# The sign of a converted weight: from a pass of its own into the slope of a Prelu

## Chip, cores and metric

The kernel runs on one core of a Trainium2 chip. The metric is the time of one execution on the device in microseconds (us). Its engines are named as in the profile: PE is TensorE's matmul queue and PEld its weight loads, DVE is VectorE, ACT is ScalarE, POOL is GpSimd, SP is SyncE, which issues the DMAs here.

## What is computed

An attention in two stages (32 packed queries per head read keys and values, then the 576 queries of a head read the packed result), whose output goes through two feed-forward layers. The weights of both layers arrive as 64-bit floats and are used as 32-bit floats.

```python
def _attn_ref(q, k, v, p):                       # 8 batches, 8 heads, 576 x 64; p has 32 rows
    p_packed = sm_attn(p, k, v)
    return sm_attn(q, p_packed, p_packed)

def _moe_ref(x, w_in, w_out):                    # x: 4608 x 512; d_ff = 2048
    h = x @ w_in
    return (h - np.tanh(h)) @ w_out

def _moe2_ref(x, w_in, w_out):
    h = x @ w_in
    return (h * np.cos(h)) @ w_out
...
    x = _moe_ref(x=x, **moe_kwargs)
    return _moe2_ref(x=x, **moe2_kwargs)
```

## The kernel before

**Stages.** First comes the attention of batch 0 and the conversion of the first weights (up to some 35 us). Then follow 128 steps of the first layer, up to some 770 us: for each half batch and each pair of hidden chunks PE makes h (`h1`, L517, 12 matmuls), ACT and DVE make h - tanh(h) of it (`el1`, `el2`, L532 to L550), `el3` (ACT, L561) and `el4` (POOL, L565) split the result into a high part gh and a low part gl, and two steps later PE multiplies both by w_out (`ymm1`, L578, 24 matmuls). The attention of the following batch is woven in between: its scores sc and their exponential e (L317, L341), transposes tp (L355), pp, s and so on, and the product gp of the packed result with w_in (`gmat`, L479), which `gsplit` (L493, L498) splits into g. The second layer with the cosine fills the rest of the time; no weight is converted there any more.

**Conversion.** `Conv` turns 64-bit floats into 32-bit floats, 64 tiles of 128 x 512 numbers in all: 32 of the first layer (16 w_in, called w1i, and 16 w_out, called wt and then w1o) up to some 165 us, and 32 of the second layer between 250 and 775 us. A tile st is loaded by SP (L149) as pairs of words. In `a`, ACT scales the high word, read as a 32-bit float, by 2^-112 (L167, Copy): that moves the exponent to the place where a shift left by 3 makes a 32-bit float of it. The sign sits in the topmost bit, and the shift pushes it out. A second ACT pass (L170) makes the three missing low bits from the low word. In `b_ops`, DVE joins both: shift left by 3, or with the low bits (`join`, L208). The sign is put back in one of two ways, chosen for each tile by the letter in `SPLIT` (first layer) and `SPLIT2` (second layer):

- "L": DVE ors the high word's sign bit into the low bits before the join (`sign`, L187). 20 tiles of the first layer, the last 8 of the second.
- "S": a third ACT pass (L175) writes the scaled high word as a 16-bit float, sign included, into the upper half of the low word. 12 tiles of the first layer, the first 24 of the second.

`c` then splits a finished w_out or second-layer tile (ACT L231, POOL L232). `gmat` needs the w1i tiles, `ymm1` the w1o tiles.

**Order.** The attention of batch 0 and, from step 15 on, all steps stand in an order written by hand. For steps 0 to 14 a scheduler orders each engine's queue by its own estimate of the durations. `STEP_A` and `CONV2` say in which steps a conversion is started; inside a step, `el2` weaves the DVE operations of pending conversions (`fill`) between its own four. On ACT a conversion started in a step stands behind that step's y and k (L539, L542) and ahead of what `mid` holds, as the exponential e.

Of the kernel before, what the change touches and what calls it, by code (L numbers as in the profile page):

```python
# [14 lines left out]
U16 = mybir.dt.uint16  # L15
U32 = mybir.dt.uint32
F16 = mybir.dt.float16
BF16 = mybir.dt.bfloat16
AF = mybir.ActivationFunctionType
ALU = mybir.AluOpType  # L20
# [13 lines left out]
    "i2 i0 i3 i1 o1 o0 i4 i5 i6 i7 o3 o4 o2 o5 o7 i8 "  # L34
    "o6 i9 i10 i11 i14 o9 i12 i13 o8 i15 o11 o13 o12 o10 o15 o14"
).split()
SPLIT = "LLSSLLSLLLSLSLSLLSLSLSLSLLSLLSLL"
SPLIT2 = "S" * 24 + "L" * 8
STEP_A = (1, 2, 2, 2, 1, 2, 1, 1, 1, 1, 0, 2, 1, 1, 1, 1, 1, 1, 0, 3, 1, 1)
CONV2 = (34, 35, 37, 38) + tuple(16 * k + r for k in (3, 4, 5, 6) for r in (0, 2, 3, 5, 6))  # L40
CONV2 += (112, 114, 116, 118, 120, 122, 124, 126)
# [29 lines left out]
    11: (13,), 12: (12, 14), 13: (15, 18, 16), 14: (19,), 16: (17,), 17: (20, 21), 18: (22,),  # L71
}
PREP0 = (23, 24, 25)
SGN = -2147483648
LOW_BIAS = -0.5 + 2.0 ** -10


# [1 line left out]
def fused_kernel(ctx, tc, qT, kT, v, pT, w1i, w1o, w2i, w2o, ident, out):  # L79
    nc = tc.nc  # L80
    B, _, _, _, HB = qT.shape
    S = 2 * HB
# [36 lines left out]
    def f32(ap):  # L119
        return ap.bitcast(F32)  # L120
# [10 lines left out]
    class Conv:  # L131
# [20 lines left out]
        def a(self):  # L152
            self.prefetch()
            if not self.ready:
                return
            kind, f, st = self.ready.pop(0)
            way = self.split[self.na]
            self.na += 1
            if kind == "w1i":
                if f // 2 not in w1in:  # L160
                    w1in[f // 2] = wp.tile([128, 2, 512], F32, tag="w", name="w1i")
                w = w1in[f // 2][:, f % 2, :]
            else:
                w = self.alloc_tmp()
            sv = st.rearrange("p (n two) -> p n two", two=2)
            hi, x = sv[:, :, 1], sv[:, :, 0]
            nc.scalar.activation(out=w, in_=f32(hi), func=AF.Copy, scale=2.0 ** -112)  # L167
            halves = st.bitcast(U16).rearrange("p (n four) -> p n four", four=4)
            if way != "D":
                nc.scalar.activation(  # L170
                    out=x, in_=x.bitcast(U32), func=AF.Identity,
                    scale=2.0 ** -29 * (1 - 2.0 ** -11), bias=LOW_BIAS,
                )
            if way == "S":
                nc.scalar.activation(  # L175
                    out=halves[:, :, 1].bitcast(F16), in_=f32(hi), func=AF.Copy, scale=2.0 ** -60
                )
            self.done_a.append((kind, f, hi, w, x, way))

        def b_ops(self):  # L180
            if not self.done_a:
                return []
            kind, f, hi, w, x, way = self.done_a.pop(0)
            wi = w.bitcast(I32)

            def sign():
                nc.vector.scalar_tensor_tensor(  # L187
                    out=x, in0=hi, scalar=SGN, in1=x, op0=ALU.bitwise_and, op1=ALU.bitwise_or
                )

            def shift():
                nc.vector.tensor_scalar(
                    out=wi, in0=wi, scalar1=3, scalar2=None, op0=ALU.logical_shift_left
                )

            def put_sign():
                nc.vector.scalar_tensor_tensor(
                    out=wi, in0=hi, scalar=SGN, in1=wi, op0=ALU.bitwise_and, op1=ALU.bitwise_or
                )

            def join():
                if way == "D":
                    nc.vector.scalar_tensor_tensor(
                        out=wi, in0=x, scalar=29, in1=wi,
                        op0=ALU.logical_shift_right, op1=ALU.bitwise_or,
                    )
                else:
                    nc.vector.scalar_tensor_tensor(  # L208
                        out=wi, in0=wi, scalar=3, in1=x,
                        op0=ALU.logical_shift_left, op1=ALU.bitwise_or,  # L210
                    )
                if kind == "w1i":
                    self.bdone.add(f)
                else:
                    self.done_b.append((kind, f, w))
                if kind[1] == "2":
                    stores.append((raw[kind[2]][f // 2][:, f % 2], w))
                self.prefetch()

            return {"S": [join], "L": [sign, join], "D": [shift, put_sign, join]}[way]  # L220

        def b(self):
            for fn in self.b_ops():
# [425 lines left out]
    def cos_round(a, h):  # L649
        nc.scalar.activation(out=a, in_=h, func=AF.Identity, bias=MAGIC)  # L650

    def cos_frac(a, h):
        nc.vector.scalar_tensor_tensor(
            out=a, in0=a, scalar=MAGIC, in1=h, op0=ALU.subtract, op1=ALU.subtract
        )
# [306 lines left out]

    conv = Conv([("w1" + o[0], int(o[1:])) for o in ORDER], 3, SPLIT, alloc_st, alloc_tmp)

# [74 lines left out]

    conv2 = Conv(todo2, 2, SPLIT2, alloc_st2, alloc_tmp2)  # L1040

# [25 lines left out]
    for n, (blk, s) in enumerate(steps):  # L1067
# [7 lines left out]
        st = {}  # L1075
# [85 lines left out]
    for s in range(NSTEP):  # L1161
        st = st0 if s == 0 else {}
# [70 lines left out]
    def psp():  # L1233
        i = nbank[0] % 4
        nbank[0] += 1
        if banks[i] is not None:
            t, banks[i] = banks[i], None
            return t
        return psx.tile([128, TB], F32, tag=f"p{i}", bufs=1, name="p")
# [78 lines left out]
    for t in pairs:  # L1318
# [23 lines left out]
        for F in range(NSTEP):  # L1342
            w = wfirst if (t, F) == (pairs[0], 0) else None
# [4 lines left out]
            A, C, B = psp(), psp(), psp()  # L1348
# [82 lines left out]
        for k, (p, P) in enumerate(jobs):  # L1431
# [7 lines left out]
            hi, lo = done[k]  # L1439
# [102 lines left out]
```

## Time and profile before

| what | value |
|---|---|
| median of 3 runs | 1495.38 us (1494.09 to 1496.17) |
| profiled execution, its own time | 1494.03 us |
| its span from first to last instruction | 1492.2 us |
| busy in the span: PE, DVE, ACT, POOL | 97%, 79%, 69%, 26% |

A page of the profile holds one execution: the busy time of each engine, the chain of work that ended last (followed back from the end, at each step to what released it), groups of instructions by line with mean duration, and waits with what ended them. A busy PE need not be PE at its peak; the granted clock is given as a share of full speed (1.00 is 2.4 GHz, 0.50 is 1.2 GHz).

### The profile page before, as it was taken

Reading aid. Unit: us, or ns where it says so; the run is one execution under the profiler, and the core shown is the slowest. Engines: PE = TensorE matmul, PEld = TensorE weight load, DVE = VectorE, ACT = ScalarE, POOL = GpSimd, SP = SyncE. Lnnn points to the kernel's source line nnn. Section 1 sums busy time; section 2 is a strip of 40 time slices with the busy share of each in tenths; the row PEclk is TensorE's granted clock in tenths of the full one; section 3 lists DMA queues with packets and bytes.
Section 4 is the critical chain, followed back from the end, with each engine's and each line's share of the span. In section 5 each row is a group of like instructions: output and inputs, shape, how many; then the busy total and the mean of one; then the engine's idle time right before and its main releaser. Section 6 shows DMA issues by size and latency. Waiting matters only on the chain.

```text
span 1492.2 us, 29411 instructions
## 1 busy us (share of the span) xinstructions
PE 1440.5 (97%) x11296; PEld 1305.9 (88%) x11296; DVE 1184.2 (79%) x1562; ACT 1034.6 (69%) x1592; POOL 383.8 (26%) x356
## 2 busy tenths in 40 slices
PE   4789999999999999999999999999999999999998
PEld 2578999989998899988998888998889988998898
DVE  6998787777878788789976778886888688868874
ACT  5899767879788787977875656655665466636652
POOL 0353454554645455454550000000000000000000
PEclk8799999999999999999999999999999999999999
DMA  9642464646647474564669757776668766776656
GB/s 356 217 159 75 144 207 139 226 143 207 211 170 246 159 246 150 198 216 151 196 244 382 247 165 231 231 254 211 206 186 255 220 203 192 237 237 205 182 161 186
DMA packets 179980, 307.67 MB, mean 206 GB/s; under 512 B 14912, under 2 KB 110144, under 8 KB 179840
## 3 DMA queue, kind: packets, MB, share of 16 engines
q1 hardware_dynamic: 179840, 305.79, 62.8%
q8 instruction: 90, 1.47, 0.4%
q14 instruction: 50, 0.41, 0.1%
HBM read 238.35 MB, written 67.37 MB: 205 GB/s over the span
## 4 chain that ended last, share of the span: by engine, by line
PE 77%; ACT 8%; DVE 5%; issue 5%; POOL 3%; DMA 1%; SPq 0%; DVEq 0%; POOLq 0%; ACTq 0%
PE p L899 21%; PE y L578 17%; PE y L909 15%; PE h L517 9%; PE p L909 6%; PE h L639 3%; PE y L715 3%; POOL gl L565 2%; PE gp L479 2%; DVE y L550 1%; ACT u L533 1%; ACT st L175 1%; ACT st L170 1%; ACT y L539 1%; DVE y L546 1%
## 5 line engine op out<-in xcount | busy, mean ns | idle before, releaser
L899 PE MATMUL p<-b,hw 128*128 128x512 f32 x1302 | 310.4, 391 | 0.0
L578 PE MATMUL y<-gh,w1o 128*128 128x288 f32 x2048 | 305.3, 301 | 3.2 <-DVE ye L608 1.0
L578 PEld LDWEIGHTS y<-gh,w1o 128*128 128x128 f32 x2048 | 279.1, 189 | 31.1 <-issue 12.0
L899 PEld LDWEIGHTS p<-b,hw 128*128 128x128 f32 x1302 | 239.1, 188 | 47.0
L565 POOL TENSOR_TENSOR gl<-y,gh 128x576 fp32r<-128x576 f32 x127 | 245.7, 1935 | 22.4 <-ACT gh L561 22.4
L517 PE MATMUL h<-a,g 128*128 128x288 f32 x1536 | 228.8, 298 | 17.8 <-DVE d L545 7.6
L517 PEld LDWEIGHTS h<-a,g 128*128 128x128 f32 x1536 | 212.9, 190 | 21.7 <-ACT st L170 8.2
L532 ACT ACTIVATE t<-h 128x576 f32<-128x576 f32 x128 | 85.3, 667 | 122.9 <-PE h L517 122.8
L578 PE MATMUL y<-gl,w1o 128*128 128x288 f32 x1024 | 157.6, 296 | 5.5 <-POOL gl L565 5.2
L578 PEld LDWEIGHTS y<-gl,w1o 128*128 128x128 f32 x1024 | 142.7, 188 | 9.2 <-POOL gl L565 8.7
L550 DVE COPY_PREDICATED y<-k,t 128x576 f32<-128x576 int16 x128 | 132.4, 1035 | 9.9
L909 PE MATMUL y<-yw,yh 128*128 128x256 f32 x768 | 136.2, 279 | 0.2 <-DMA yw<-wod 0.2
L544 DVE TENSOR_TENSOR t<-h,t 128x576 f32<-128x576 f32 x128 | 95.2, 744 | 51.2 <-ACT u L533 50.7
L909 PEld LDWEIGHTS y<-yw,yh 128*128 128x128 f32 x768 | 117.6, 188 | 0.9 <-ACT o L920 0.4
L546 DVE SCALAR_TENSOR_TENSOR y<-y,d 128x576 f32<-128x576 f32 x128 | 104.0, 813 | 16.9 <-ACT y L539 10.4
L909 PE MATMUL y<-yw,yl 128*128 128x256 f32 x384 | 107.4, 280 | 0.0
L917 DVE TENSOR_TENSOR yl<-k,yh 128x1024 fp32r<-128x1024 f32 x72 | 87.1, 1220 | 23.4 <-ACT yh L920 22.9
L561 ACT ACTIVATE gh<-y 128x576 fp32r<-128x576 f32 x128 | 88.2, 689 | 9.9 <-DVE y L550 9.6
L545 DVE TENSOR_TENSOR d<-u,h 128x576 f32<-128x576 f32 x128 | 94.9, 742 | 0.0
L909 PE MATMUL y<-yw,gh 128*128 128x256 f32 x512 | 94.0, 280 | 0.0
L909 PE MATMUL p<-yw,yh 128*128 128x256 f32 x512 | 91.0, 279 | 0.0
L920 ACT ACTIVATE c<-p 128x512 f32<-128x512 f32 x96 | 56.9, 593 | 47.7 <-PE p L899 47.7
(166 smaller groups left out, 2609.1 us busy)
## 6 DMA issues: line engine op xcount, KB each, us to landing
yw<-wso SPq DMA_DIRECT2D x128, 256.0 KB, 3.0
hw<-wsi SPq DMA_DIRECT2D x124, 256.0 KB, 3.0
w1i<-w1d SPq DMA_DIRECT2D x48, 512.0 KB, 5.2
yw<-wod SPq DMA_DIRECT2D x96, 256.0 KB, 3.3
hw<-wid SPq DMA_DIRECT2D x93, 256.0 KB, 3.2
y<-ye SPq DMA_DIRECT2D x80, 144.0 KB, 1.9
st<-w1i SPq DMA_DIRECT2D x16, 512.0 KB, 8.4
v<-vv SPq DMA_DIRECT2D x16, 512.0 KB, 6.7
```

Of the source, the lines that this page charges most:

```text
L517: nc.tensor.matmul(out=h[:, x, 0:HB], lhsT=gw[b, f // 4, half][:, ga, c0:c0 + 128], rhs=a2[b, half][:, aa, HB * j:HB * j + HB], start=(n = ...
L532: nc.scalar.activation(out=st["t"], in_=h, func=AF.Tanh)
L544: lambda: nc.vector.tensor_tensor(out=t, in0=hs, in1=t, op=ALU.subtract),
L545: lambda: nc.vector.tensor_tensor(out=d, in0=u, in1=hs, op=ALU.mult),
L546: lambda: nc.vector.scalar_tensor_tensor(out=y, in0=y, scalar=PC0 - PC1 * PC1 / (4 * PC2), in1=d, op0=ALU.add, op1=ALU.mult,),
L550: lambda: nc.vector.copy_predicated(out=y, mask=k.bitcast(I16), data=t),
L561: nc.scalar.activation(out=st["gh"], in_=st["g"], func=AF.Copy)
L565: eng.tensor_tensor(out=st["gl"], in0=st["g"], in1=f32(st["gh"]), op=ALU.subtract)
L578: nc.tensor.matmul(out=yps[blk][d][:, 0:HB], lhsT=w1out[f][:, wh, 128 * d:128 * d + 128], rhs=st[gg][:, x, :], start=(s in first and x == ...
L899: nc.tensor.matmul(out=dst, lhsT=w[:, wi, 128 * j:128 * j + 128], rhs=b[j][bi], start=(first and n == 0), stop=(n == 5), skip_group_check= ...
L909: nc.tensor.matmul(out=dst[m // 2][:, 256 * (m % 2):256 * (m % 2) + 256], lhsT=src[:, 128 * m:128 * m + 128], rhs=w[:, wi, :], start=(firs ...
L917: nc.vector.tensor_tensor(out=out, in0=x, in1=y, op=op)
```

## The change

ACT's scaling pass becomes a Prelu with the same scale and a slope of 2^32 for negative words. A negative word comes out with its exponent raised by 32, which sets the exponent bit that the join's shift by 3 moves to the place of the sign. The weights' scaled exponents are below 32, so that bit is clear in a positive word. With that neither the DVE pass `sign` nor the third ACT pass is needed: each of the 64 tiles takes two ACT passes and one join. The way "D", which was not used, becomes "V" and is not used either.

```diff
-SPLIT = "LLSSLLSLLLSLSLSLLSLSLSLSLLSLLSLL"
-SPLIT2 = "S" * 24 + "L" * 8
+SPLIT = "A" * 32
+SPLIT2 = "A" * 32
...
-            nc.scalar.activation(out=w, in_=f32(hi), func=AF.Copy, scale=2.0 ** -112)
-            halves = st.bitcast(U16).rearrange("p (n four) -> p n four", four=4)
-            if way != "D":
+            nc.scalar.activation(
+                out=w, in_=f32(hi), func=AF.Prelu, scale=2.0 ** -112, alpha=2.0 ** 32
+            )
+            if way == "A":
                 nc.scalar.activation(
                     out=x, in_=x.bitcast(U32), func=AF.Identity,
                     scale=2.0 ** -29 * (1 - 2.0 ** -11), bias=LOW_BIAS,
-                )
-            if way == "S":
-                nc.scalar.activation(
-                    out=halves[:, :, 1].bitcast(F16), in_=f32(hi), func=AF.Copy, scale=2.0 ** -60
                 )
...
-            def sign():
-                nc.vector.scalar_tensor_tensor(
-                    out=x, in0=hi, scalar=SGN, in1=x, op0=ALU.bitwise_and, op1=ALU.bitwise_or
-                )
...
-            return {"S": [join], "L": [sign, join], "D": [shift, put_sign, join]}[way]
+            return {"A": [join], "V": [shift, join]}[way]
```

The lines behind move up by 14 (one less ahead of the join): L166 is the Prelu now, L194 the join, L518 the tanh that was L532, and so on. Both programs load two activation tables, at the same places.

On ACT, at the start of the steps, behind the split of the first g (L493, now L479). Before, with the e of batch 1 (L341), the first tanh (L532) and its square:

```order
L493 ACTIVATE g<-gp 128x512 x2
L167 ACTIVATE w1i<-st 128x512
L170 ACTIVATE st<-st 128x512
L341 ACTIVATE e,sm<-sc,nm 128x576
L175 ACTIVATE st<-st 128x512
L167 ACTIVATE w1i<-st 128x512
L170 ACTIVATE st<-st 128x512
L231 ACTIVATE w1o<-wt 128x512
L170 ACTIVATE st<-st 128x512 x2
L532 ACTIVATE t<-h 128x576
L533 ACTIVATE u<-h 128x576
```

And now:

```order
L479 ACTIVATE g<-gp 128x512 x2
L166 ACTIVATE w1i<-st 128x512
L170 ACTIVATE st<-st 128x512
L166 ACTIVATE w1i<-st 128x512
L170 ACTIVATE st<-st 128x512
L327 ACTIVATE e,sm<-sc,nm 128x576
L217 ACTIVATE w1o<-wt 128x512 x2
L166 ACTIVATE w1i<-st 128x512
L170 ACTIVATE st<-st 128x512
L518 ACTIVATE t<-h 128x576
L519 ACTIVATE u<-h 128x576
```

The half-word pass is gone, the second w1i tile stands ahead of e, and two w1o splits ahead of the third.

On PE, behind the 12 matmuls of the first h, with the second gp (L479, now L465). Before:

```order
L479 MATMUL gp<-w1i,pt 32x256 x16
L355 MATMUL tp<-idn,e 128x128 x4
L355 MATMUL tp<-idn,e 64x128
L317 MATMUL sc<-k,pin_145 32x288 x8
L578 MATMUL y<-gh,w1o 128x288 x9
L517 MATMUL h<-a_399,g 128x288
```

And now:

```order
L465 MATMUL gp<-w1i,pt 32x256 x12
L341 MATMUL tp<-idn,e 128x128 x4
L341 MATMUL tp<-idn,e 64x128
L465 MATMUL gp<-w1i,pt 32x256 x4
L303 MATMUL sc<-k,pin_145 32x288 x8
L564 MATMUL y<-gh,w1o 128x288
L503 MATMUL h<-a_395,g 128x288
```

The last four of the sixteen gp matmuls have moved behind the transposes, and eight of nine y matmuls behind the second h.

On DVE, in a step near 710 us, where the second layer's last tiles are converted (way "L"). Before:

```order
L544 TENSOR_TENSOR t<-h,t 128x576
L545 TENSOR_TENSOR d<-u,h 128x576
L187 SCALAR_TENSOR_TENSOR st<-st 128x512
L546 SCALAR_TENSOR_TENSOR y<-y,d 128x576
L208 SCALAR_TENSOR_TENSOR wt<-wt,st 128x512
L550 COPY_PREDICATED y<-k,t 128x576
```

And now:

```order
L530 TENSOR_TENSOR t<-h,t 128x576
L531 TENSOR_TENSOR d<-u,h 128x576
L194 SCALAR_TENSOR_TENSOR wt<-wt,st 128x512
L532 SCALAR_TENSOR_TENSOR y<-y,d 128x576
L536 COPY_PREDICATED y<-k,t 128x576
```

The join has moved up into the place of the sign pass, ahead of y.

## Rows read from the trace of the kernel before

**Rows 1.** Page, part 1: busy us, share of the span, instructions of each engine.

```profile
PE 1440.5 (97%) x11296; PEld 1305.9 (88%) x11296; DVE 1184.2 (79%) x1562; ACT 1034.6 (69%) x1592; POOL 383.8 (26%) x356
```

**Rows 2.** Stretches: length; busy us PE, PEld, DVE, ACT, POOL; clock, DMA share, GB/s.

```profile
30.00:150.00 120.00, 98.19 (x889) 84.14 (x890) 108.46 (x151) 108.94 (x190) 50.59 (x49) 0.89 0.46 165
...
250.00:690.00 440.00, 433.99 (x4216) 402.67 (x4215) 353.12 (x537) 355.93 (x621) 233.82 (x212) 1.00 0.57 196
800.00:1200.00 400.00, 399.37 (x2405) 356.51 (x2404) 318.18 (x366) 240.78 (x293) 0.00 (x0) 1.00 0.73 230
```

**Rows 3.** PE's waits up to 150 us: total us, times, longest.

```profile
PE h L517 <- DVE d L545: 5.2, 4, 2.3
```

**Rows 4.** Chain of work that ended last, 30 to 150 us, shares by line.

```profile
by line: issue 15.1%; DVE y L550 9.6%; ACT st L170 7.1%; DVE y L546 5.5%; ACT st L175 5.3%; ACT y L539 4.3%; ACT u L533 3.8%; DVE t L544 3.7%; DVE st L187 3.7%; ACT gh L561 3.5%; PE h L517 3.3%; ACT g L493 3.3%; ACT wt L167 3.2%; PE y L578 
```

**Rows 5.** Lines L167, L175, L187: duration ns minimum/median/maximum, first and last start.

```profile
L167 ACT ACTIVATE wt<-st x48: 648/669/710, 25.2 to 763.5; 128x512 f32<-128x512 f32 x48
...
L175 ACT ACTIVATE st<-st x36: 1326/1384/1435, 18.5 to 637.4; 128x512 f16<-128x512 f32 x36
...
L187 DVE SCALAR_TENSOR_TENSOR st<-st x28: 650/684/1786, 14.5 to 772.1; 128x512 int32<-128x512 int32 x28
```

**Rows 6.** Chain that ended last, in order of time: start us, us, what.

```profile
14.48 0.70 DVE st L187
...
23.35 1.35 ACT st L175
...
35.10 1.26 ACT st L175
...
40.61 0.68 DVE st L187
...
47.67 0.68 ACT gh L561
```

**Rows 7.** Timeline, 22 to 36 us: start, us, engine, line, tiles [idle before].

```profile
24.73 0.69 DVE L208 SCALAR_TENSOR_TENSOR w1i<-w1i,st 128x512 int32<-128x512 int32 x1 [0.46 <-ACT st L175]
...
34.74 1.54 PE L517 MATMUL h<-a,g 128*128 128x288 f32 x5 [7.34 <-DVE g L498]
```

**Rows 8.** Groups by line, 30 to 150 us: count, busy us, mean ns, idle before.

```profile
L170 ACT ACTIVATE st<-st 128x512 int32<-128x512 uint32 x24 | 16.1, 688 | 0.0
L175 ACT ACTIVATE st<-st 128x512 f16<-128x512 f32 x10 | 13.7, 1366 | 0.0
...
L187 DVE SCALAR_TENSOR_TENSOR st<-st 128x512 int32<-128x512 int32 x16 | 15.0, 935 | 1.1 <-ACT st L170 1.0
```

**Rows 9.** PE's waits, 250 to 690 us.

```profile
PE h L517 <- DVE d L545: 1.9, 3, 0.7
...
PE sc L317 <- ACT e L341: 1.5, 3, 0.5
```

**Rows 10.** Timeline, 602 to 605 us: ACT and PE around e.

```profile
602.44 1.38 ACT L175 ACTIVATE st<-st 128x512 f16<-128x512 f32 x1
603.56 0.74 ACT L341 ACTIVATE e<-sc,nm 128x576 f32<-128x576 f32 x1
...
604.43 0.72 PE L317 MATMUL sc<-k,pin 64*32 64x288 f32 x16 [0.49 <-ACT e L341]
```

**Rows 11.** Timeline, 547 to 552 us: half-word pass, and DVE's wait behind the square.

```profile
547.73 1.38 ACT L175 ACTIVATE st<-st 128x512 f16<-128x512 f32 x1
...
550.15 0.76 DVE L544 TENSOR_TENSOR t<-h,t 128x576 f32<-128x576 f32 x1 [1.64 <-ACT u L533]
```

**Rows 12.** PE's waits, 690 to 776 us.

```profile
PE y L578 <- POOL gl L565: 3.5, 5, 1.1
```

**Rows 13.** Timeline, 705 to 713 us: L550 at once behind y, and behind a join.

```profile
705.04 0.83 DVE L550 COPY_PREDICATED y<-k,t 128x576 f32<-128x576 int16 x1
...
711.31 2.04 DVE L550 COPY_PREDICATED y<-k,t 128x576 f32<-128x576 int16 x1
...
712.73 1.33 PE L578 MATMUL y<-gl,w1o 128*128 128x288 f32 x8 [0.55 <-POOL gl L565]
```

More of the change, by code (lines that the diff above doesn't have):

```diff
@@ L73 @@
 PREP0 = (23, 24, 25)
-SGN = -2147483648
 LOW_BIAS = -0.5 + 2.0 ** -10
@@ L194, in shift @@
                 )
[L196 to L199, printed above, removed]
             def join():
-                if way == "D":
+                if way == "V":
                     nc.vector.scalar_tensor_tensor(
```

## The prediction

> **What bounds the kernel now.** I read the page's busy shares first: TensorE (PE) is busy 97% of the span [rows 1], so little can be gained where it runs without a break. The table by stretches says where that is [rows 2]. From 800 to 1200 us PE is busy 399.37 of 400 us; no conversion stands there, and I leave everything behind 776 us at its present length. From 250 to 690 us it is busy 433.99 of 440 us. From 30 to 150 us it is busy only 98.19 of 120 us, part of it at the lower granted clock (0.89 of full on the mean, 1.00 in the later stretches), while VectorE (DVE) is busy 108.46 us and ScalarE (ACT) 108.94 us. That stretch belongs to DVE and ACT together. The waits agree: PE stands idle for DVE, 5.2 us in four waits for d alone up to 150 us [rows 3]. The chain of work there is a mixture of both engines, and the two kinds of instruction that the change deletes stand on it: the half-word pass L175 with 5.3% and the sign pass L187 with 3.7% of 120 us, so 6.4 and 4.4 us [rows 4].
>
> **The change part by part.** Each of the 64 conversions keeps its scaling pass, its low-word pass and its join. Deleted are 36 ACT passes L175 with a median of 1384 ns, some 50 us of ACT, and 28 DVE passes L187 with a median of 684 ns, some 19 us and more where they are stretched (the longest took 1786 ns) [rows 5]. Twelve L175 and 20 L187 belong to the first layer, all started by 165 us; 24 L175 lie between 250 and 640 us, 8 L187 between 690 and 775 us. No DMA is added or taken away, and no wait is added: Prelu takes the place of the Copy, with the same operand and the same wait for its load.
>
> **Prelu's price** is not in the trace. The nearest row is the Copy that it replaces, with the same shape, strides and immediates: 669 ns at the median, 648 at the shortest [rows 5]. Above it stands the Identity pass L170 (scale and bias immediate), 688 ns on the mean in the crowded stretch [rows 8], and far above L175 with 1384 ns. I take 0.67 us, so no gain or loss. A table load would cost extra, but the built order has the same two as before, at the same places.
>
> **Up to 30 us.** The chain charges 0.70 us to the first L187 and 1.35 us to the second L175 [rows 6]. Not all of that comes back: behind the L175, DVE had stood idle for only 0.46 us before the join [rows 7], since it had its own work until then, and px must wait for its matmuls. From that join DVE and then ACT run almost without a gap to the first h at 34.74 us [rows 7]. I count 0.5 us, a quarter of the 2.05 charged.
>
> **30 to 150 us.** The chain charges 10.8 us to the two passes (above). To see how much returns I walked the new ACT and DVE rows with today's durations over the first step. In 34 to 48 us the chain charges 1.26 and 0.68 us; in the new order the last w1i word of the second gp is joined at about 41.3 us, and gh of the first step stands at 46.0 instead of 47.67 us [rows 6]: 1.7 of 1.94 us return, some 85%. PE's order helps a little beyond that: the second h stands behind one y matmul instead of nine. So 0.85 x 10.8 = 9.2 us. The low end is the quarter that the first 30 us keep, 2.7 us. The high end takes both engines' remaining work at today's share of busy time: ACT 108.9 - 13.7 (ten L175 of 1366 ns), DVE 108.5 - 15.0 (sixteen L187 of 935 ns) [rows 8]; ACT is the larger with 95.3 us, at 0.908 busy 104.9 us instead of 120: 15.1 us.
>
> One thing speaks for less. The sixteen L187 average 935 ns in this stretch against a median of 684 [rows 5, 8]: some were held up while GpSimd (POOL) was at work. If that hold passes to the next DVE instruction, only 16 x 0.68 = 10.9 us of DVE is freed, and of the chain's 4.4 us about 1.0 stays, which would make 8.3 of the 9.2 us. The Trainium skill (SBUF — State Buffer, section "SBUF: two separate sides") says so as a rule: GpSimd and a DVE instruction with two SBUF inputs take turns at a shared port pair, held for a whole instruction; the longest L187, 1786 ns [rows 5], fits it. By it I would forecast 0.9 us less; I leave it in the range.
>
> **250 to 690 us.** PE waits 1.5 us for the exponential e (three times) and 1.9 us for d (three times, the longest 0.7 us) [rows 9]. At the first kind, L175 (602.44, 1.38 us) stands directly ahead of e on ACT, and PE starts sc only when e ends, after 0.49 us of idling [rows 10]. Without L175, e starts 1.12 us earlier and the wait is gone. At the second kind, L175 (547.73) stands ahead of the tanh on ACT, DVE idles 1.64 us for the square behind it, and h waits for d behind it [rows 11]; it goes too, and so does its twin near 371 us. The longest of the three has no L175 ahead of it and stays. That is 1.5 + 1.9 - 0.7 = 2.7 us, with the refill of PE's pipe about 3.0. Waits for POOL's gl there follow a DVE backlog without sign passes and stay. Range 2 to 4 us.
>
> The Trainium skill (ScalarE: Activation LUTs, section "What ACT_TABLE_LOAD costs") gives an ACTIVATE with immediates 186 ns + 0.833 ns per element: by it L175 with 512 elements would take an estimated 0.61 us. The rows show 1.38 us [rows 5], and the row decides. By the page's figure the 36 passes would be worth 22 us instead of 50, and the whole gain about 10 us.
>
> **690 to 776 us.** Here PE waits 3.5 us in five places, all for gl [rows 12], one of them 0.55 us at 712.73 [rows 13]. The join moves into the sign pass's place ahead of y, so y, and POOL's gl behind it, start no earlier within the step. What changes stands behind y. Today the join lets gl begin first, and L550 beside it takes 2.04 us (711.31); where L550 follows y at once, it takes 0.83 us (705.04) [rows 13]. So each of these steps frees 0.68 us and up to 1.2 us more of DVE, and the next step's t starts earlier; that is what the three waits between 705 and 724 us (1.1, 0.55 and 0.5 us) hang on. The last two waits come from POOL's own queue. At most 2.2 us, against some 0.3 us by which gl is slower when L550 goes first; I take 1.7, range 0.5 to 2.5.
>
> **Sum.** 0.5 + 9.2 + 3.0 + 1.7 = 14.4 us off the profiled execution's 1494.03 us (its span of 1492.2 and 1.8 around it): 1479.6. That execution lies 1.35 us under the median of the runs, 1495.38, so against the median the forecast is 1481.
>
> **Rivals.**
> (a) *The conversion is mostly beside the path in the start.* The elementwise work of the steps fills the gaps, and the first 150 us give back only the low ends, 0.5 + 2.7; with 3.0 and 1.7 later that is 7.9 us, 1487. For it: the first 30 us. Against it: both engines are at 90% and both are relieved.
> (b) *Nothing moves.* If Prelu took two passes' time, 1.38 us, ACT would change by 24 x 0.71 - 13.7 = +3.3 us in 30 to 150 us (24 conversions there [rows 8]) and DVE alone would gain; the start would come out about even, and the middle keeps under 3 us: around 1493. The same form and operands speak against it.
> (c) *Slower: the new order holds PE up.* In the first fifteen steps a scheduler orders the engines. It now places the last four gp matmuls behind the transposes, and parts of y of an earlier step ahead of a later h. An h that stands behind a y whose gl or weight is late idles, as PE does now behind d, up to 2.3 us at a time [rows 3]. To end 3 us slower than today these new waits would have to eat the 14.4 us and 3 more, seven or eight waits of 2.3 us in fifteen steps; that is 1498. Against it: the moved matmuls are those whose operands the shorter conversion makes ready earlier.
>
> **How the numbers follow.** A run of this kernel can tell about 0.2%, 3 us, from no change. I give the forecast (a gain of 10 to 18 us) 0.60, more than that 0.07, rival (a) 0.20, rival (b) 0.08, rival (c) 0.05. The first three are all faster by over 3 us: 0.87. Rival (b) is within 3 us: 0.08. Slower: 0.05. The range adds the ends: at best 0.5 + 15.1 + 4 + 2.5 = 22 us off 1495.4, so 1473, and 1472 with rounding; at worst 0.5 + 2.7 + 2 + 0.5 = 5.7 off, so 1490.
>
> **What would show it.** Prelu at 0.65 to 0.70 us a piece and no third table load; ACT's busy time down by some 50 us and DVE's by 19 to 25; the first gh near 46 us, and the work that now ends at 150 us done some ten us earlier; no PE wait for e after 250 us; the gl waits in 690 to 776 us down to under 2 us, with L550 near 0.83 us there; the part behind 776 us as long as now. It is wrong if Prelu takes over 0.8 us, if the start gains under 4 us although both engines' work shrank, or if PE shows new waits of a microsecond or more behind gp or y in the first 150 us.

## The result, and the profile after

The changed kernel runs in 1483.83 us (median of 4 runs, 1482.44 to 1484.11), the kernel before in 1495.76 us beside it: 0.992 of its time, 95% interval 0.990 to 0.994, so 11.9 us faster. The forecast was 1481 us in a range of 1472 to 1490, faster. The profiled executions took 1494.03 and 1483.77 us, 10.3 us apart; that of before lies 1.7 us under its median, that of after at its own. The forecast from profile to profile was 14.4 us, so some 4 us of it did not come by the profiles, and 2.5 by the medians. The measured 1483.8 lies halfway between the forecast and rival (a)'s 1487.

Part 1 of the page of the changed kernel (busy us, share, instructions), which answers [rows 1]:

```profile
PE 1437.3 (97%) x11296; PEld 1305.4 (88%) x11296; DVE 1159.2 (78%) x1534; ACT 993.0 (67%) x1556; POOL 385.4 (26%) x356
```

DVE has lost its 28 instructions and 25.0 us, ACT its 36 instructions, but 41.6 us instead of the 50 forecast. The three stretches of [rows 2] now (length; busy us of PE, PEld, DVE, ACT, POOL; clock, DMA share, GB/s):

```profile
30.00:150.00 120.00, 101.01 (x941) 88.33 (x941) 100.53 (x141) 101.92 (x188) 54.42 (x51) 0.96 0.50 174
250.00:690.00 440.00, 436.68 (x4243) 406.40 (x4242) 358.83 (x539) 332.79 (x606) 236.15 (x214) 1.00 0.56 195
800.00:1200.00 400.00, 399.38 (x2415) 356.92 (x2414) 317.20 (x361) 242.46 (x297) 0.00 (x0) 1.00 0.71 224
```

A stretch of fixed length holds more work when a kernel is faster, so the two programs are better compared at marks of the program. The mark taken here is the start of a step's tanh on ACT (L532, now L518); the lead is how much earlier it comes:

| start of the tanh of step | before, us | lead of after, us | gained since the mark above | forecast |
|---|---|---|---|---|
| 0 | 38.94 | -0.2 | -0.2 | 0.5, and a part of the 9.2 |
| 17 | 154.85 | 5.5 | 5.7 | 9.2 |
| 33 | 246.0 | 5.4 | 0 | 0 |
| 115 | 704.6 | 9.3 | 3.8 | 3.0 |
| 127 | 764.8 | 11.0 | 1.7 | 1.7 |
| end of the span | 1492.2 | 10.2 | -0.8 | 0 |

So the later stages came out as forecast or above it, and the start, up to step 17, gave 5.5 us instead of 9.7. These are figures of one execution each: two kernels that run the same instructions up to a mark can reach it 1.3 us apart (`second_only` below, at step 0), though steps 0 to 16 took 115.9 us in the kernel before and 115.5 in `second_only`. To see where the start fell short, it is cut at steps 0, 3, 8, 12 and 17. First the kernel before, then the changed one (columns as above):

```profile
38.94:63.26 24.32, 18.14 (x196) 13.86 (x193) 21.55 (x36) 23.48 (x41) 7.14 (x8) 0.71 0.61 203
63.26:103.32 40.06, 33.33 (x272) 28.73 (x278) 38.66 (x49) 34.05 (x60) 25.05 (x22) 0.95 0.58 209
103.32:123.96 20.64, 19.87 (x194) 18.22 (x193) 19.44 (x27) 20.21 (x38) 6.14 (x9) 1.00 0.31 108
123.96:154.85 30.89, 27.51 (x266) 24.94 (x272) 24.65 (x33) 26.39 (x50) 13.43 (x14) 1.00 0.17 45
```

```profile
39.15:62.46 23.31, 17.32 (x189) 13.24 (x189) 19.06 (x31) 20.54 (x38) 9.29 (x8) 0.85 0.71 246
62.46:97.12 34.66, 30.58 (x260) 27.50 (x266) 33.42 (x46) 30.42 (x55) 22.44 (x20) 0.95 0.60 218
97.12:118.44 21.32, 21.25 (x207) 20.03 (x207) 17.50 (x22) 18.27 (x34) 6.76 (x9) 1.00 0.30 104
118.44:149.38 30.94, 27.09 (x261) 24.28 (x267) 23.65 (x31) 24.60 (x47) 13.04 (x14) 1.00 0.19 48
```

The four rows read differently. In steps 0 to 2 ACT was busy 23.48 of 24.32 us; it lost 2.9 us, the time only 1.0. In steps 3 to 7 DVE was busy 38.66 of 40.06 us and is busy 33.42 of 34.66 now: it is full in both kernels, it lost 5.2 us, and the time lost 5.4. (A DVE instruction that is held up beside POOL counts as busy here.) In steps 8 to 11 PE has gone from 19.87 of 20.64 to 21.25 of 21.32: it has no idle time left, and the stretch is 0.7 longer, since more matmuls fall into it. Steps 12 to 16 are as long as before.

The chain of work of the kernel before, cut at the same marks, charged the two deleted passes with:

| part | L175 and L187 in the chain of before, us | came off, us |
|---|---|---|
| 30 us to step 0 | 1.3 | -0.2 (up to step 0) |
| steps 0 to 2 | 2.0 | 1.0 |
| steps 3 to 7 | 5.6 | 5.4 |
| steps 8 to 11 | 2.0 | -0.7 |
| steps 12 to 16 | 0 | 0 |

In steps 3 to 7, where DVE was full, as much came off as the chain had charged; elsewhere less came off than was charged. The 5.6 us there are 3.0 of sign passes on DVE and 2.5 of half-word passes on ACT, which was busy only 34.05 of 40.06 us, so a full DVE alone does not account for all of it. `late_stores` below does the same conversion work, and there 2.4 us came off in these steps.

### The profile page after: what moved, and what is told of

The parts are those of the page before. It is cut to its first block, busy times and chain, and to the rows that moved or that the text cites. A ratio compares the mean times of both kernels' runs of the same rounds, so it can differ in the third digit from the quotient of the medians.

```text
span 1482.0 us, 29370 instructions
## 1 busy us (share of the span) xinstructions
PE 1437.3 (97%) x11296; PEld 1305.4 (88%) x11296; DVE 1159.2 (78%) x1534; ACT 993.0 (67%) x1556; POOL 385.4 (26%) x356
## 4 chain that ended last, share of the span: by engine, by line
PE 82%; issue 4%; DVE 4%; POOL 3%; DMA 3%; ACT 3%; SPq 0%; DVEq 0%; POOLq 0%; ACTq 0%
PE p L885 21%; PE y L564 20%; PE y L895 15%; PE h L503 10%; PE p L895 6%; PE h L625 3%; PE y L701 3%; POOL gl L551 2%; DMA st<-w1i 2%; PE gp L465 2%; DVE y L536 1%; DVE y L532 1%; ACT u L519 1%; DMA q<-qT 1%; PE s L303 1%
## 5 line engine op out<-in xcount | busy, mean ns | idle before, releaser
L518 ACT ACTIVATE t<-h 128x576 f32<-128x576 f32 x128 | 83.4, 651 | 146.6 <-PE h L503 146.6
L536 DVE COPY_PREDICATED y<-k,t 128x576 f32<-128x576 int16 x128 | 125.4, 980 | 11.1 <-DVE y L532 0.5
L532 DVE SCALAR_TENSOR_TENSOR y<-y,d 128x576 f32<-128x576 f32 x128 | 104.8, 818 | 18.3 <-ACT y L525 12.1
L525 ACT ACTIVATE y<-u 128x576 f32<-128x576 f32 x128 | 87.7, 685 | 3.6 <-POOL gl L551 2.6
```

Of the source, the lines that this page charges most:

```text
L525: nc.scalar.activation(out=y, in_=u, func=AF.Square, scale=PC2 ** 0.5, bias=PC1 / (2 * PC2 ** 0.5))
L532: lambda: nc.vector.scalar_tensor_tensor(out=y, in0=y, scalar=PC0 - PC1 * PC1 / (4 * PC2), in1=d, op0=ALU.add, op1=ALU.mult,),
L536: lambda: nc.vector.copy_predicated(out=y, mask=k.bitcast(I16), data=t),
```

## Experiments

All times are medians beside runs of the kernel before on the same chip (1495.1 to 1495.9). Theories: **P**, both engines share the path in the start, and each us removed gives back a part of itself; **B**, one engine was the bound and the path has left it; later **D**, the loads are what stands behind; **A**, the attention of batch 1 is a gate; **E** and **F**, none of these two, the work of the steps themselves.

### Which half of the change, and which layer

`second_only` puts the old ways back into the first layer, `first_half` and `first_sign` change only its 12 "S" or its 20 "L" tiles (all three also bring back the code of the old ways, left out here):

```diff
 # second_only
-SPLIT = "A" * 32
+SPLIT = "LLSSLLSLLLSLSLSLLSLSLSLSLLSLLSLL"
 # first_half: "S" becomes "A", the sign pass stays on the "L" tiles
+SPLIT = "LLAALLALLLALALALLALALALALLALLALL"
 # first_sign: "L" becomes "A", the half-word pass stays on the "S" tiles
+SPLIT = "AASSAASAAASASASAASASASASAASAASAA"
...
```

> The 32 first-layer tiles go back to the two old ways (a third ACT pass for 12, a DVE sign pass for 20, Copy as the scaling pass); the 32 second-layer tiles keep the Prelu. In the changed kernel the lead over the kernel before was 5.5 us when the last first-layer tile was done and 10.2 us at the end, so what lies behind is worth 4.7 us. If the two halves are independent: 1495.8 - 4.7 = 1491 us. If the later gain depends on the earlier start (later stages begin at another point of the loads): anything but that, up to 1495.

> In the first layer only the 12 tiles with the third ACT pass are changed (that pass goes, some 16.6 us of ACT); 20 tiles keep their DVE sign pass; second layer as in the changed kernel. Theory P (both engines share the path, and each us removed gives back the same part of itself): 12 x 1.38 us of ACT against 20 x 0.68 and stretch, some 17 us, of DVE, so half of the first layer's 5.5 to 7 us: about 1487.5. Theory B (one engine was the bound, and behind it stands something else, loads or the steps' own chain): if that engine is ACT, nearly all of the gain, 1484 to 1485; if it is DVE, nearly none, 1490 to 1491.

> In the first layer only the 20 tiles with the DVE sign pass are changed (it goes); 12 tiles keep their third ACT pass; second layer as in the changed kernel. Theory P: about 1487.5, and the gains of this run and of the one with only the ACT passes removed add up to that of both. Theory B: 1484 to 1485 if DVE was the bound, 1490 to 1491 if ACT was; the two gains do not add up.

Measured: 1488.95 us (1488.24 to 1489.42), 1486.03 (1485.37 to 1486.95) and 1487.10 (1485.72 to 1488.45), beside 1495.27. The second layer alone is worth 6.3 us, more than the 4.7 read from the two profiles. (Its profiled execution was 1.3 us late at step 0, where it runs the same instructions as the kernel before; from there to the end it gained 6.2.) Against it the first layer's half-word passes are worth 2.9 us, its sign passes 1.85, both together 5.1 (5.6 if each kernel is held against the runs of the kernel before beside it). The two add up to 4.8, within the spread of the runs, as P has it, and B falls in both forms.

Where each of them acts shows in the same cuts, steps 0 to 2 and 3 to 7. `first_half`:

```profile
39.22:61.85 22.63, 17.72 (x192) 13.68 (x185) 19.38 (x34) 19.86 (x37) 9.27 (x7) 0.98 0.83 295
61.85:99.75 37.90, 32.74 (x267) 29.40 (x273) 37.80 (x50) 31.59 (x59) 25.03 (x23) 0.92 0.57 208
```

`first_sign`:

```profile
39.49:65.22 25.73, 17.51 (x184) 14.07 (x185) 19.05 (x32) 23.89 (x41) 8.01 (x9) 0.82 0.70 247
65.22:100.88 35.66, 31.88 (x268) 28.62 (x274) 31.61 (x45) 33.47 (x59) 23.57 (x21) 0.94 0.53 191
```

Without the half-word passes steps 0 to 2 are 1.7 us shorter (24.32 before); steps 3 to 7 are 2.2 shorter and stay under DVE, busy 37.80 of 37.90 us (38.66 before). Without the sign passes steps 3 to 7 are 4.4 us shorter, and steps 0 to 2 are 1.4 longer, with ACT busy 23.89 of 25.73. So ACT's relief is what counts in the first steps, and DVE's counts most in the next five. That neither pays for half of its charge (2.9 of 6.4 us, 1.85 of 4.4) fits such a mixture; how much of each is due to the order that the scheduler chose anew for each kernel was not separated.

### What more ACT relief would give

`no_low` also leaves out the first layer's low-word pass, `no_low_both` that of both layers (`SPLIT2` too):

```diff
-SPLIT = "A" * 32
+SPLIT = "T" * 32
...
             def join():
-                if way == "V":
+                if way == "T":
+                    shift()
+                elif way == "V":
```

> The changed kernel, in which the first layer's 32 conversions also lose their low-word pass: the join becomes a shift of one operand, and the three lowest bits of the weights stay zero. Some 16.4 us of ACT go between 30 and 150 us. Theory P, at the rate that the change itself gave back in the start (5.5 us for 13.7 of ACT and 15.0 of DVE): 16.4 x 0.19 = 3.1 us, 1480.7. Theory B: the path has left the conversion for the loads and the steps' own chain, under 1 us, 1483 to 1484.

Measured: 1481.76 us (1481.16 to 1481.87), 2.1 less than the changed kernel, between P's 3.1 and B's under 1. Steps 0 to 2 and 3 to 7:

```profile
38.08:59.13 21.05, 16.25 (x184) 13.25 (x177) 17.36 (x31) 15.78 (x29) 7.35 (x6) 0.84 0.71 246
59.13:95.83 36.70, 31.11 (x259) 27.65 (x265) 32.46 (x45) 25.46 (x47) 23.35 (x21) 0.92 0.63 224
```

ACT is down to 25.46 of 36.70 us in steps 3 to 7, and these are 2.0 us longer than in the changed kernel. Its gain lies in steps 0 to 2 (2.3 us) and at step 0 (1.1). So more relief for ACT is worth something up to step 3 and nothing in the five steps behind. The edit relieves DVE a little too: the shift alone took 0.41 us where nothing disturbed it, the join 0.68.

> The changed kernel without the low-word pass in both layers: the join is a shift of one operand, and the three lowest bits of all converted weights stay zero. Against the run that did so in the first layer alone (1481.76 us) 32 more ACT passes of 0.67 us go between 250 and 776 us, 21 us of ACT. In the changed kernel PE waits there for no ACT result; it waits for POOL's gl (1.7 us in 250 to 690, 2.0 behind) and 0.7 us for one d. Theory P, at the first layer's 0.13 us per us of ACT: 2.8 us, 1479. Theory W (only passes directly ahead of a wait count; none is left there): within 0.6 of 1481.8.

Measured: 1480.73 us (1480.37 to 1482.14), 1.0 less than `no_low`, though their ranges overlap; neither theory's number, and closer to W's. What fell is PE's wait for gl: from 1.7 to 1.2 us in 240 to 680 us, and behind it, from 680 to 766 us, from 2.0 to 1.3:

```profile
PE y L566 <- POOL gl L553: 1.3, 3, 0.6
```

A reading of this is that the wait hangs on DVE, whose shift (L183) averages 557 ns there where the join averaged 822, and not on the ACT pass; the run changes both at once, so it is not shown. This kernel is the fastest of all measured, by 3.1 us against the changed one, and pays with three bits of every converted weight.

### Are the loads what stands behind in the start?

In the changed kernel ACT waits for a load in the first steps, and two stores stand ahead of that load on SP. `late_stores` and `before_late_stores` move the stores, in the changed kernel and in the one before; `o_not_loaded` takes other loads away:

```diff
 # late_stores, before_late_stores
-W1STORE = {8: 0, 9: 1, 10: 2, 11: 3, 16: 4, 17: 5, 18: 6, 19: 7}
+W1STORE = {18: 0, 19: 1, 20: 2, 21: 3, 22: 4, 23: 5, 24: 6, 25: 7}
 # o_not_loaded
-                nc.sync.dma_start(out=st, in_=srcs[kind][f].bitcast(I32))
+                if kind == "w1o" and f in (1, 0):
+                    nc.gpsimd.memset(f32(st), 1.0)
+                else:
+                    nc.sync.dma_start(out=st, in_=srcs[kind][f].bitcast(I32))
```

> The changed kernel, in which the eight stores of the first layer's w_in tiles (512 KB each), that later batches read back, are written in steps 18 to 25 instead of 8 to 19. In the changed kernel four of them stand on SP's queue ahead of or among the first loads (issued at 25.94, 26.36, 37.16 and 42.41 us) while the DMAs are busy 0.96 of the time up to 30 us; the load of the seventh w_in tile behind them lands at 38.0, and ACT waits 0.69 us for it. Theory D (the start now waits for loads): 1 MB less ahead of that load, 2.5 us at 400 GB/s, of which ACT's own work leaves 1 to 2 us: 1482 to 1483 us. Theory E (the loads are beside the path, the steps' own chain and the engines' work set the pace): 1483.8, within 0.6.

> The kernel before with the same later stores. There the seventh w_in tile was scaled at 40.52 us, 12.6 us after its load was issued, and no ACT instruction behind 28 us waited for a load. Theory D: ACT and DVE were late anyway, no gain, 1495.3 within 0.6. Should the stores cost time for another reason (a store waits on SP for its join, and loads stand behind it), both kernels gain the same 1 to 2 us.

> The changed kernel without the loads of the first two w_out tiles (1 MB): GpSimd, idle until 36 us, fills them with a constant, so the output is not the reference's; all passes on ACT and DVE stay, in the same order on ACT. Theory D: the next four w_in tiles land some 2.5 us earlier; the second gp stops waiting for its last tiles, and 1 to 2.5 us come off: 1481.5 to 1483. Theory E: 1483.8, within 0.6.

Measured: 1484.47 us (1483.79 to 1486.61), 1495.60 (beside 1495.92; interval of the ratio 0.9988 to 1.0005) and 1482.48 (1482.04 to 1483.55). The load does stand where D says. ACT in the changed kernel, at the seventh w_in tile and at gh of step 0:

```profile
38.01 0.68 ACT L166 ACTIVATE w1i<-st 128x512 f32<-128x512 f32 x1 [0.69 <-DMA st<-w1i]
...
47.34 0.68 ACT L547 ACTIVATE gh<-y 128x576 fp32r<-128x576 f32 x1 [0.49 <-DVE nm L320]
```

and in `late_stores`:

```profile
36.11 0.69 ACT L166 ACTIVATE w1i<-st 128x512 f32<-128x512 f32 x1
...
46.03 0.68 ACT L547 ACTIVATE gh<-y 128x576 fp32r<-128x576 f32 x1
```

With the load early gh stands at 46.03 us, which is the 46.0 of the prediction's walk. But it brings nothing at the end. At step 4 `late_stores` leads the changed kernel by 2.3 us, at step 8 it is 0.4 behind. Its steps 3 to 7:

```profile
59.85:97.53 37.68, 31.64 (x262) 28.36 (x268) 36.40 (x47) 30.81 (x56) 24.17 (x21) 0.92 0.53 181
```

3.0 us longer than in the changed kernel, with DVE busy 36.40 of 37.68: what came earlier in the first steps ran into DVE. DVE runs one instruction more there than in the changed kernel (47, 46); most of its extra 3.0 us are longer instructions, the joins of two w_out tiles at 1558 ns on the mean instead of 678 above all. So a stretch of five steps moves by 2 to 3 us with the order alone: `before_late_stores`, whose conversion is the old one, took 37.78 us in steps 3 to 7 against 40.06, and 25.80 in steps 0 to 2 against 24.32. `o_not_loaded` shows the same in small: its seventh w_in tile was scaled at 37.25 without a wait and its first tanh came 0.75 us earlier, but from step 3 to step 127 it stands within 0.15 us of the changed kernel at every mark above. Its median is 1.3 us lower, its profiled execution 0.2; which of the two is the edit's stays open. D falls as the cause of the missing 4 us; it holds for the first steps alone.

### Is batch 1's attention a gate?

PE waits three times at the first h of step 8, the first that needs batch 1's attention result a and its g. PE's matmuls there in the changed kernel:

```profile
92.29 0.40 PE L503 MATMUL h<-a,g 128*128 128x288 f32 x1 [0.91 <-ACT a L415]
...
93.34 0.40 PE L503 MATMUL h<-a,g 128*128 128x288 f32 x1 [0.53 <-DVE g L484]
...
95.62 1.46 PE L503 MATMUL h<-a,g 128*128 128x288 f32 x9 [0.69 <-DVE g L484]
```

Two kernels take h's need away (in the changed kernel and in the one before), two ask for a or g earlier:

```diff
 # b1_not_waited, before_b1_not_waited
-        b, j = divmod(blk, 2)
+        b, j = divmod(0 if blk == 2 else blk, 2)
 # g_earlier: the first number of G1; att_earlier_ls: all three, and late_stores
-G0, G1, G = (0, 14, 12), (7, 8, 15, 22), (9, 11, 13, 15)
+G0, G1, G = (0, 14, 12), (6, 8, 15, 22), (9, 11, 13, 15)
-ATT1 = ((-2, 0, 1, 4), (0, 1, 2, 5))
+ATT1 = ((-2, 0, 1, 4), (0, 1, 2, 4))
-LOAD1 = (-7, -2, -1, 0, -4, 4)
+LOAD1 = (-7, -2, -1, 0, -4, 3)
```

> The changed kernel, in which steps 8 to 11 (the first half of batch 1) multiply with batch 0's attention result and g; batch 1's are still made, by the same instructions, but no step waits for them before step 12, so the output is not the reference's. In the changed kernel the first h of step 8 waits for them: a was finished at 94.3 us, g at 95.6, PE idles 2.7 us between 90.98 and 95.62 in three waits, and the lead over the kernel before falls there from 7.5 us (start of step 6) to 5.5 to 6.2 (steps 7 and 8). Theory A (that chain is a gate: what the conversion gives back ahead of it is held there): without the gate 2 to 3 us come off, 1481 to 1482 us. Theory F (the engines' work in every step sets the pace, the gate is incidental): within 0.7 of 1483.8.

> The kernel before with the same edit (steps 8 to 11 multiply with batch 0's attention result and g, so the output is not the reference's). There a of batch 1 was finished at 102 us and PE idled 2.3 us for it and g. Theory A: some 1 to 2 us come off here too, 1493.5 to 1494.5, but less than in the changed kernel: the difference between the two kernels without the gate is 12 to 13 us instead of 11.5. Theory F: within 0.7 of 1495.5.

> The changed kernel with the product of batch 1's packed result and w_in (gp, and its split into g) asked for in step 6 instead of 7, ahead of the last step of batch 0. In the changed kernel gp was done at 86.2 us, but ACT split it only at 90.35, behind a step's tanh, square, gh, y and k, and DVE ended g at 95.6. Theory A: g is ready before a (94.3), the wait falls by 1.3 us: 1482.5. Theory F: within 0.7 of 1483.8.

> The changed kernel with three moves that leave the work as it is: the second half of batch 1's attention starts in step 4 instead of 5 (its q is loaded a step earlier), its gp stands in step 6 instead of 7, and the w_in stores are late (steps 18 to 25). With late stores alone the lead was 7.35 us at step 4 (5.05 without) and gone at step 8. Theory A: with the gate a step earlier that part stays, 1480 to 1482 us. Theory F: the same work in a tighter place, 1483.5 to 1486.

Measured: 1482.51 us (1482.02 to 1483.65), 1494.04 (1492.34 to 1494.68), 1485.17 (1483.59 to 1488.14) and 1484.29 (1483.76 to 1484.73), beside 1495.13. Where no h waits, the changed kernel's median is 1.3 us lower and that of the kernel before 1.1, the latter at the edge of the noise (interval of its ratio 0.9982 to 1.0000); the two kernels are 11.5 us apart, with the wait 11.9. So A's 2 to 3 us and its 12 to 13 us between the kernels did not come. But the edit moved the wait more than it took it away. The three waits above are 2.1 us (not 2.7, as expected there), and without them PE stood 2.9 us at gp for the same g (1.5 us in the kernel before with this edit):

```profile
95.38 1.10 PE L465 MATMUL gp<-w1i,pt 64*32 64x256 f32 x32 [2.92 <-DVE g L484]
```

So no run shows that batch 1's attention holds back what the conversion gave, and none rules it out. In the changed kernel without h's need the lead at step 8 is 8.0 us and at step 12 6.1. PE is busy 22.52 of 22.56 us in steps 8 to 11, with 207 matmuls as in the 21.32 us of the changed kernel, but at a granted clock of 0.92 on the mean instead of 1.00:

```profile
95.34:117.90 22.56, 22.52 (x207) 21.55 (x207) 18.43 (x23) 19.43 (x37) 7.79 (x9) 0.92 0.29 98
```

Asking for g a step earlier is slower in four of five runs than the changed kernel's median; both theories missed that. Its trace has the lead at step 7 down to 3.6 us: between steps 6 and 7 PE waits 2.11 us for a d, and the 12 matmuls of h behind that wait take 3.17 us at a granted clock of 0.50, where those of the step ahead took 1.76. Whether the earlier gp brought this about stays open.

## Why the prediction was right, and where it was not

**What bounds the kernel.** Right in the large: PE is the bound behind 776 us and nothing was gained there (PE is still busy 399.38 of 400 us from 800 to 1200). 0.8 of the 11.0 us of lead went lost behind 765 us: the lead is 11.4 us at 780, falls by 0.3 near 1170 and 1320 us and by 0.5 behind the last matmul. The cause stays open; in the other kernels, which run the same instructions there, this loss lies between 0 and 1.1 us.

**Prelu's price.** Forecast 0.67 us and no third table load. Groups of ACT in the changed kernel (line, count, busy us, mean ns, idle before):

```profile
L166 ACT ACTIVATE wt<-st 128x512 f32<-128x512 f32 x48 | 32.2, 671 | 1.4 <-DMA st<-w1o 1.4
L166 ACT ACTIVATE w1i<-st 128x512 f32<-128x512 f32 x16 | 10.7, 669 | 0.7 <-DMA st<-w1i 0.7
...
L952 ACT ACT_TABLE_LOAD x1 | 1.3, 1283 | 0.7 <-PEq L1518 0.7
L1118 ACT ACT_TABLE_LOAD x1 | 1.3, 1283 | 0.0
```

671 and 669 ns against the Copy's median of 669 [rows 5], and two table loads. Rival (b) fell with it. That ACT's busy time sank by 41.6 and not 50 us is an error of the sum: 36 x 1384 ns counts each pass to its end, but the next one starts before that (L175 started at 34.98 in the kernel before, and L167 behind it at 36.09, 1.11 us later). 41.6 / 36 is 1.16 us a pass. The Trainium skill (ScalarE: Activation LUTs, section "What ACT_TABLE_LOAD costs") says that ACTIVATEs in a row overlap by some 93 ns; the rows show 0.11 us behind a Prelu (33.23 to 33.78 for one of 0.66) and 0.27 behind that L175 of 1.38.

**Up to 30 us, and 30 to 150 us.** Here lies the term that was mis-sized: "0.85 x 10.8 = 9.2 us", and 0.5 ahead of it; both together gave 5.5 us by the profiles, 5.1 to 5.6 by the runs (`second_only` and the changed kernel). The 10.8 us that the chain charges are no error; the 0.85 is. It came from walking the new order over one step, 34 to 48 us, and was laid on 120 us. Even in that step it failed: gh came at 47.34 us, not at 46.0, because the walk left the loads out, and with the stores out of the way it did come at 46.03. But that was not the cause of the loss, since it brought nothing at the end. What the cuts show is that the stretch is four stretches with different limits. In steps 3 to 7, under DVE, 5.4 us came off beside a charge of 5.6. In steps 0 to 2 ACT lost 2.9 us and the time a third of that. In steps 8 to 11 PE took over at once, and 2.0 us of charge brought nothing. That these limits are the cause is read from the traces; no run isolates it. Rows that were at hand pointed this way: PE was busy 98.85 of the 115.91 us between steps 0 and 17, so 9.2 us would have been more than half of its 17.1 us of idle time there, and in steps 8 to 11 only 0.8 us were to be had. (Of the 5.7 us that came off, 3.1 are idle time and 2.6 busy time; the latter has twelve matmuls fewer in it, which moved across the marks, and a mean granted clock of 0.95 instead of 0.92. The two were not separated.) The result lies between the forecast's 9.2 and rival (a)'s 2.7, and (a)'s reason, that conversion fills gaps, fits steps 12 to 16, where nothing was charged and nothing came off.

What PE waits for in the first 150 us has changed its kind (total us, times, longest):

```profile
PE y L564 <- ACT gh L547: 3.1, 2, 2.7
PE gp L465 <- DVE d L531: 3.0, 2, 1.7
PE gp L465 <- DVE w1i L194: 1.7, 2, 1.2
...
PE h L503 <- DVE d L531: 1.2, 2, 0.6
PE tp L341 <- DVE d L531: 1.2, 1, 1.2
```

and two of these waits in the kernel before:

```profile
PE y L578 <- ACT gh L561: 0.5, 2, 0.3
PE gp L479 <- DVE d L545: 0.5, 1, 0.5
```

Waits for d were 5.2 us in h alone [rows 3], and are 5.4 in h, gp and tp now. Some of this is what rival (c) feared, new waits behind gp and y of over a microsecond (the longest 1.7 and 2.7 us, where gp had waited 0.5 for d and y at most 0.3 for gh); they ate a part, not the whole. The prediction had named such waits as a sign of being wrong. That sign came; gh stood at 47.3 instead of near 46 us, and 5.5 instead of some ten us were won by 150 us. So the time lies in the range, but what the prediction said of the start was in part wrong.

**The hold beside POOL.** The prediction saw that sign passes are stretched where POOL works, and counted 0.9 us if that passes on to the next DVE instruction. At one place the trace shows it passing on. Joins of w1i in steps 3 to 7 of the changed kernel, and the longest of them, with PE's wait behind it:

```profile
L194 DVE SCALAR_TENSOR_TENSOR w1i<-w1i,st 128x512 int32<-128x512 int32 x7 | 8.5, 1228 | 0.2 <-ACT st L170 0.2
```

```profile
80.59 3.05 DVE L194 SCALAR_TENSOR_TENSOR w1i<-w1i,st 128x512 int32<-128x512 int32 x2
...
85.11 1.10 PE L465 MATMUL gp<-w1i,pt 64*32 64x256 f32 x32 [1.75 <-DVE d L531]
```

Five joins of w1i in steps 3 to 7 of before took 1028 ns on the mean, and the two ahead of t and d in step 6 there 0.68 and 0.67 us. In the changed kernel the two ahead of t and d in step 6 take 3.05 us together, PE waits 1.75 us for that d, and between steps 6 and 7 the lead falls from 7.5 to 5.5 us. In `late_stores`, `first_half` and `first_sign` it does not fall there. How much of the hold passes on in all is not settled. DVE's time above its undisturbed durations (the lower fifth of those of the same form) is an estimated 16.8 us from 30 to 150 us before and 14.2 after, but 15.5 in `second_only`, which has the same sign passes as before, and 17.2 in `late_stores`, which has none. The rule of the Trainium skill (SBUF — State Buffer, section "SBUF: two separate sides") agrees with the trace here: the joins, the copy L536 and y (L532) are the ones that are longer beside POOL, and t and d, which read one input from PSUM, are not (746 and 741 ns on the mean from 30 to 150 us). The 0.9 us is a part of the missing 4 by estimate; no run isolated it.

**250 to 690 us.** Forecast 3.0 (2 to 4), measured 3.8. PE's waits, which answer [rows 9], and behind them those of 690 to 776 us [rows 12]:

```profile
PE y L564 <- POOL gl L551: 1.7, 3, 0.8
PE sc L303 <- PE h L503: 0.8, 1, 0.8
PE h L503 <- DVE d L531: 0.7, 1, 0.7
```

```profile
PE y L564 <- POOL gl L551: 2.0, 4, 0.8
```

No wait for e is left, two of three for d are gone and the longest, 0.7, has stayed, as the prediction said. The lead steps up by 0.57 us near 339, 426 and 605 us (the e's) and by 1.0 near 375 and 550 (the d's), 3.7 us in five steps. The waits alone were 0.5 and 0.6. The rest is PE's busy time: over the five steps around 371 us the same 270 matmuls kept PE busy 27.99 us in the kernel before and 27.66 in the changed one, and over the five around 334 us 262 matmuls 27.77 and 27.69. The prediction put this down to the refill of PE's pipe and counted some 0.3 us in all; it comes to about 0.9, and no run shows what it is.

**690 to 776 us.** Forecast 1.7, measured 1.7, with the wait for gl at 2.0 us and not under it. The mechanism is the forecast one: the copy that follows y at once takes 0.83 us beside POOL's gl, which takes the 2.03. Of the three waits for gl between 705 and 724 us that of 1.1 is gone and that of 0.53 down to 0.16, but that of 0.55 has grown to 0.84 us, by the 0.3 that the prediction had set against the gain. DVE and POOL in the step of [rows 13]:

```profile
710.48 0.83 DVE L536 COPY_PREDICATED y<-k,t 128x576 f32<-128x576 int16 x1
710.53 2.03 POOL L551 TENSOR_TENSOR gl<-y,gh 128x576 fp32r<-128x576 f32 x1
```

## What to carry to other kernels

A chain's charge for an instruction is no price list: here as much as charged came off where DVE was full and nothing where PE had next to no idle time, and with another order of the same work less than half of it came off under the same full DVE. Cut a long stretch at marks of the program, read which engine is full in each part, and hold the gain that you expect there against the idle time of the engine that bounds the whole. A shortening walked over one step is a bound for that step and no rate for the rest: here 1.3 us won at one place (the late load) were gone by step 8. And two reliefs of different engines in such a mixture pay a part each, so do not drop the one that looks like the smaller.

## What the runs showed of the hardware

A low granted clock cost nothing over steps in which PE waited. `second_only` runs the same first layer as the kernel before. In 36 to 60 us the kernel before was granted 0.70 of full speed on the mean (1.2 GHz from 23.3 to 50.6 us, 2.4 behind that; PE had been busy 15.92 of the first 30 us and idle 7.3 us ahead of the first h), `second_only`, whose PE had been busy 16.78 of the first 30 us and idle as long ahead of its first h, 1.00 (2.4 GHz throughout):

```profile
36.00:60.00 24.00, 18.20 (x195) 12.77 (x193) 21.70 (x37) 23.18 (x40) 6.14 (x5) 0.70 0.61 201
```

```profile
36.00:60.00 24.00, 19.02 (x190) 13.85 (x190) 21.88 (x38) 23.16 (x41) 6.20 (x5) 1.00 0.60 203
```

Steps 0 to 2 lasted 24.32 us in the one, at 0.71 on the mean, and 24.37 in the other, at 0.95.

Where PE's matmuls stood in a row, they took longer at the low clock. Sixteen matmuls of y in two neighbouring steps of the changed kernel, at 2.4 GHz and, granted 0.51 from 86.5 to 90 us, at 1.2 GHz nearly throughout:

```profile
78.43 2.28 PE L564 MATMUL y<-gh,w1o 128*128 128x288 f32 x16
...
86.14 3.92 PE L564 MATMUL y<-gh,w1o 128*128 128x288 f32 x16
```

What such a drop costs a whole execution was not separated from what else moved.

A one-input DVE instruction is held beside POOL as well. The shift that takes the join's place in `no_low`, one operand and 32-bit words, took 0.41 us alone and 1.50 beside POOL's w1o split:

```profile
56.19 0.41 DVE L183 TENSOR_SCALAR w1i<-w1i 128x512 int32<-128x512 int32 x1
...
64.69 1.50 DVE L183 TENSOR_SCALAR w1i<-w1i 128x512 int32<-128x512 int32 x1
```

And steps 12 to 16, with four conversions started in them, lasted 30.8 to 31.0 us in all the kernels, whatever their conversions did.
